# Linear-attention block with a gated MLP, on one core: operands' stages in the order of the products, wo's splits ahead of their matmuls, loads moved in the queue

## The chip, the core and the metric

One of the eight cores of a Trainium2 chip runs the whole program. The time is that of one launch on the device, in microseconds (us): the median of 3 runs of the kernel before is 2439.75 us (2436.82 to 2441.01). Engines are named as in the profile: PE is TensorE (matmuls; PEld its weight loads), DVE is VectorE, ACT is ScalarE, POOL is GpSimd, SP is SyncE, whose queue here issues nearly all loads.

## The reference

All tensors are float32; S = 2048 tokens, D = 1024, F = 3584, 32 heads of 32.

```python
xn   = layernorm(x)
q, k, v = heads(xn @ wqkv)                       # D x 3D
pq, pk  = phi(q), phi(k)                         # phi(t) = (t > 0 ? t + 1 : exp(t)) + 1e-6
kv   = einsum("bhsd,bhse->bhde", pk, v)
z    = pk.sum(over s)
o    = (pq @ kv) / (pq . z + 1e-6)
s    = rows(o) @ wo                              # D x D
h    = silu(xn @ w1) * (xn @ w3)                 # D x F each
out  = x + s * silu(h @ w2)                      # F x D
```

## The kernel before, in words

**Products.** A float32 operand is split by `split` (L79) into a high part, cast by ACT (L83), and the rest, subtracted by DVE (L84). `mm3` (L88) makes a product of three matmuls (L91 high × high, L92 high × low, L93 low × high). Each 2 × 2 block of a matrix product takes seven products in place of eight: the weights' operands are B11, T2, T3, T1, B21, T4, B22 in this order (`PRODUCTS`), with T1 = B12 − B11, T2 = B22 − T1, T3 = B22 − B12, T4 = B21 − T2, the activations' partners A11, S2, S3, S1, A12, A22, S4. One product of a projection is 12 matmuls of 128 × 512.

**The first era.** The tokens go in two halves of 1024. For each half `half` (L517) runs the groups k and v, then q, then gate and up (`g`, `u`; 14 pairs); `gemm` (L393) runs the seven products of one group and the sums on the results, such as c22 (L430, L436). Two groups can be run side by side, product by product (`paired`): the last gate/up pair of half 0 and the first k/v pair of half 1.

**What sets the order.** The code is traced in an order, and a scheduler then places the instructions by that order as a priority and by its own model of times; buffers come from pools with a fixed number of slots. Three streams are traced between the products of `gemm`:

- `next(stages)`, one stage a product: the stages of `Operands` (L281), which load a group's weights (raw tile, tag "raw") and make its seven split operands in the pool tag "b", of 8 slots. `ready` (L313) splits, `combine` (L319) subtracts in place over a raw quarter. `ask` (L292) loads; a group asks for the next group's weights as its own stages begin.
- `catch_up` (L381), one step of a job a product. In half 1 the jobs are `attention_work`: the denominators, `merge_wo` (for each of 8 row tiles of wo: multiply by the masked kv sums `kvm`, then the sums and the seven operands stored to `wp_d`), and `divide` (queries divided by the denominators, stored to `qs_d`). A job flagged `in_order` is issued no earlier than the loads in `fetched`.
- use of the results (`hidden`, `keys_values`): silu, the gate, stores to `h_d`, and sums stored to `hs_d`.

**Attention and layers.** A `Segment` holds seven operands of weights for each k (`right`) and runs over 8 groups m of 256 tokens. Attention multiplies the divided queries by `wp` (o @ wo merged), whose raw tiles `wpr` go through 2 buffers (loaded in `attention_right`, L1020). `operands(m + 1)` loads the queries (`left`, L953, 4 slots of tag "sg") while m runs. m = 0 takes each k's products as they land (`outer`). `late_work` (divide for m = 6 and 7) is the job of this phase. Then era 1's pools are closed and the layers B0 to B4 multiply h by w2 in the same way; their first raw tiles (`rB11B`, `rT2B`, ..., loaded at L970) use `small` (tag "c", 6 slots).

Names in the profile: `wos` is a split half of a wo tile, `wp` both the result of the merge (in the matmuls of L776) and attention's split operand; `XA11s` and so on are split queries; a trailing `s` or `B` stands for attention and a layer.

Of the kernel before, what the change touches and what calls it, by code (L numbers as in the profile page):

```python
# [16 lines left out]
P = 128  # L17
C = 512
# [4 lines left out]
def tile_linear_attention_times_swiglu(  # L23
# [27 lines left out]
    def bank(name):  # L51
        return ps.tile([P, C], F32, tag="bank", name=name)
# [228 lines left out]
    class Operands:  # L281
# [2 lines left out]

        def __init__(self, w, c0, name, early=False):
            self.w, self.c0, self.name, self.raw, self.next = w, c0, name, None, None
            self.B, self.places = {}, {}
            self.stages = self.made(early)  # L290

        def ask(self):  # L292
# [9 lines left out]
        def made(self, early):  # L302
            K = ND // 2
            b = {}

            def halves(t):
                b.update(B11=t[:, :K, :P], B21=t[:, K:, :P])

            def place(n):
                self.places[n] = pb.tile([P, 2, K, P], FR, tag="b", name=f"{n}{self.name}")  # L310

            def ready(n):
                if n not in self.places:  # L313
                    place(n)
                split(self.places[n], b[n])
                self.B[n] = self.places[n]
# [12 lines left out]
            self.ask()  # L329
            if self.next and not early:  # L330
                self.next.ask()
            halves(self.raw)
            b.update(B12=self.raw[:, :K, P:], B22=self.raw[:, K:, P:])
            if not early:
                ready("B11")
                yield
            combine("T1", "B12", "B11", "B11")
            ready("T1")
            if early:
                combine("T2", "B22", "T1", "T1")  # L340
                ready("T2")
            yield
            if not early:
                place("T2")
            combine("T3", "B22", "B12", "B12")
            ready("T3")
            yield
            if not early:
                ready("B21")
                yield  # L350
                combine("T2", "B22", "T1", "T1")
                ready("T2")
                yield
            combine("T4", "B21", "T2", "T2")
            ready("T4")
            yield
            ready("B22")
            yield

    def in_turn(groups):  # L360
# [393 lines left out]
    def merge_wo(k):  # L754

        both = []

        def load(e):
            j = k + e * (ND // 2)
            t = job_tile([P, 2, C], f"wo{j}")  # L760
            nc.sync.dma_start(out=t, in_=wo[j * P:(j + 1) * P, :].rearrange("p (n c) -> p n c", c=C))
            return t

        def steps(e, t):
            both.append(t)
            j = k + e * (ND // 2)
            f = small(f"kvf{j}")[:, :P]
            nc.vector.tensor_mul(f, hmask, kvacc[:, j])
            kvm = st.tile([P, 2, P], FR, tag="kvm", bufs=1, name=f"kvm{j}")
            split(kvm, f)  # L770
            for n in range(2):
                o = pb.tile([P, 2, C], FR, tag="b", name=f"wos{j}_{n}")
                split(o, t[:, n])
                yield True
                acc = bank(f"wp{j}_{n}")
                mm3(acc, (kvm[:, 0], kvm[:, 1]), (o[:, 0], o[:, 1]), True, True)  # L776
                nc.scalar.copy(out=t[:, n], in_=acc)
            yield True
            if e:
                b = [t[:, n] for t in both for n in range(2)]  # L780
                for n, i in (("B11", 0), ("B21", 2), ("B22", 3)):
                    store(n, b[i])
                yield from sums_of(*b)
                for n, i in (("T1", 0), ("T3", 1), ("T4", 2), ("T2", 3)):
                    store(n, b[i])
                for _ in range(3):
                    yield True

        def store(n, t):
            g, e = divmod(7 * k + PRODUCTS.index(n), 4)  # L790
            nc.sync.dma_start(out=wp_d[g][:, e], in_=t)

# [18 lines left out]

    groups = []
    for h in range(NH):
        some = [Operands(wqkv, part * D + pair * 2 * P, f"{'qkv'[part]}{h}_{pair}_", h == 0 and part and pair < 2)
                for parts in ((1, 2), (0,)) for pair in range(ND // 2) for part in parts]
        some += [Operands((w1, w3)[e], pair * 2 * P, f"{'gu'[e]}{h}_{pair}_") for pair in range(NF // 2) for e in range(2)]
# [7 lines left out]
    stages = in_turn(groups)  # L824
    for h in range(NH):
        half(h)
    jobs.append((late_work(), False))


    GT = 2 * P  # L830
# [106 lines left out]
    def left(m, g, halves, sums, nk, name, first=False):  # L937
# [7 lines left out]
        for e, n in enumerate(PRODUCTS):  # L945
            n = PARTNER[n]
            if first:
                if e % 2 == 0:
                    big = job_tile([P, 2, nk, P], f"r{e}{name}_{m}")
                t = big[:, e % 2]  # L950
            else:
                t = signed(f"r{n}{name}_{m}")[:, :nk * P].rearrange("p (k s) -> p k s", s=P)
            nc.sync.dma_start(out=t, in_=where[n])  # L953
            yield n, t

    def queries(m):
# [5 lines left out]
    def hiddens(i, m):  # L962
# [2 lines left out]
        return left(m, m % NT, [h_[:, :, e] for e in range(2)], [hs[:, :, e] for e in range(2)],  # L965
                    (FB[i][1] - FB[i][0]) // 2, f"B{i}")

    def second_weights(i, n, k):
        t = small(f"r{n}B{i}_{k}")
        nc.sync.dma_start(out=t, in_=second_weight(i, n, k))  # L970
        return t

    def second_weight(i, n, k):
        f0, f1 = FB[i]
# [16 lines left out]
        nc.vector.tensor_add(a, a, xs)  # L991
        nc.gpsimd.dma_start(out=out[r0:r0 + P, cols], in_=a)

    def run(seg, nxt=None, around=None):

        def between(k):
            if m == NG - 1 and nxt:
# [9 lines left out]
        for m in range(NG):  # L1007
            if m + 1 < NG:
                seg.operands(m + 1)
            seg.tokens(m, m == 0 or m == NG - 1 and nxt is not None, between)  # L1010


# [17 lines left out]
    attention.operands(0)  # L1030
    for k in range(attention.nk):
        attention.right(k)
    run(attention)
    assert all(next(j, None) is None for j, _ in jobs)
    jobs.clear()
    era1.close()
# [2 lines left out]
    def layer_place(n, i, k):  # L1039
# [36 lines left out]
```

## Time and profile before

| | |
|---|---|
| median of 3 runs | 2439.75 us |
| the profiled execution | 2441.47 us |
| its span, mean granted clock of PE | 2439.7 us, 0.988 |
| projections, gate and up | to about 1690 us; border of the halves near 840 |
| merging wo | within 1135 to 1300 us |
| attention | about 1690 to 1862 us |
| layers | from about 1862 us |
| DMA over the span | 408.63 MB, mean 167 GB/s |

A timeline row gives start, duration, engine, line, operation, out<-in, shapes, and in brackets the idle time before it with what ended it. `SPq` is SP's queue: the row is the issue of a load, which lands later. Two matmuls overlap, so a row of 0.39 us is followed by the next after 0.23.

### The profile page before, as it was taken

The numbers are of one execution on the slowest core, as the hardware profiler recorded it, in microseconds if no ns is written. First come the engines' busy times: TensorE is split into PE (matmuls) and PEld (weight loads), VectorE is DVE, ScalarE is ACT, GpSimd is POOL, SyncE is SP. The second block draws the span as 40 slices with busy tenths as digits, with TensorE's granted clock in tenths as the row PEclk, the third lists the DMA queues.
The fourth block names the chain that finished last, engine by engine and source line by source line (L and its number), as shares of the span: only waits on it lengthen the run. The fifth ranks groups of instructions, "written<-read, shape, count | busy, mean of one in ns | idle before, by whom it ended". The sixth has DMA issues, their size and how long they took to land.

```text
span 2439.7 us, 30863 instructions
## 1 busy us (share of the span) xinstructions
PE 2349.5 (96%) x10544; PEld 1934.8 (79%) x10544; DVE 1823.4 (75%) x2688; ACT 937.1 (38%) x1667; POOL 726.4 (30%) x909
## 2 busy tenths in 40 slices
PE   6999999999999999999989999999898999999997
PEld 5788888788888788887767888888686888777875
DVE  8655888888887755567778877888555776776797
ACT  4434644433233243354333323333323434343433
POOL 3000012256765200011324443234330032323253
PEclk9999999999999999999999999999999999999999
DMA  3211455576667731133455555457776445454597
GB/s 122 86 52 61 149 172 171 173 226 222 224 202 238 256 141 53 52 117 127 134 186 168 198 191 203 137 193 241 242 234 195 140 139 157 122 160 119 169 292 235
DMA packets 375134, 408.63 MB, mean 167 GB/s; under 512 B 19840, under 2 KB 308608, under 8 KB 374976
## 3 DMA queue, kind: packets, MB, share of 16 engines
q1 hardware_dynamic: 348800, 319.35, 42.2%
q0 software_dynamic: 26176, 87.31, 9.6%
q8 instruction: 82, 1.34, 0.2%
q14 instruction: 76, 0.62, 0.1%
HBM read 268.96 MB, written 137.63 MB: 167 GB/s over the span
## 4 chain that ended last, share of the span: by engine, by line
PE 50%; DVE 5%; DMA 4%; issue 3%; ACT 2%; POOL 0%; DVEq 0%; POOLq 0%; ACTq 0%; SPq 0%
PE dB L91 1%; PE dB L93 1%; PE dB L92 1%; DMA wpr<-wp_d 1%; PE cB L91 1%; PE cB L93 1%; PE cB L92 1%; PE aB L93 1%; PE aB L91 1%; PE aB L92 1%; PE den L713 1%; PE kv L506 1%; DMA rB11B<-in_B_w 1%; PE cs L92 1%; PE as L92 1%
## 5 line engine op out<-in xcount | busy, mean ns | idle before, releaser
L614 POOL DMA_DIRECT2D h_d<-sg x112 | 61.6, 550 | 364.3 <-DVE sg L613 359.9
L575 POOL DMA_DIRECT2D pq_d<-pq x32 | 17.4, 545 | 484.1 <-DVE pq L467 484.0
L912 POOL TENSOR_TENSOR acc<-acc,uB 128x512 f32<-128x512 f32 x25 | 41.6, 1665 | 157.7 <-DVE uB L909 157.7
L596 POOL TENSOR_TENSOR qd<-qd 128x128 f32<-128x128 f32 x32 | 25.2, 788 | 144.7 <-DVE qd L745 139.5
L889 POOL TENSOR_TENSOR acc<-acc,uB 128x512 f32<-128x512 f32 x7 | 11.7, 1676 | 147.0 <-ACT uB L881 147.0
L600 POOL TENSOR_TENSOR hs<-sg,hs 128x256 f32<-128x256 f32 x56 | 52.9, 945 | 1.6
L597 POOL TENSOR_TENSOR hs<-hs,sg 128x256 f32<-128x256 f32 x56 | 47.2, 842 | 0.0
L628 POOL TENSOR_TENSOR w<-w 128x256 f32<-128x256 f32 x28 | 26.0, 929 | 68.7 <-DMA w<-in_B_w 63.4
L982 POOL DMA_DIRECT2D s_d<-s x32 | 17.4, 544 | 94.1 <-DVE s L919 41.6
L599 POOL TENSOR_TENSOR hs<-sg 128x256 f32<-128x256 f32 x56 | 42.8, 765 | 0.0
L596 POOL TENSOR_TENSOR hs<-sg,sg 128x256 f32<-128x256 f32 x56 | 42.5, 759 | 1.0
L91 PE MATMUL cB<-T,XA22B 128*128 128x512 f32 x87 | 34.9, 401 | 7.5 <-DVE acc L916 7.2
L914 POOL TENSOR_TENSOR acc<-acc,uB 128x512 f32<-128x512 f32 x25 | 40.2, 1610 | 0.0
L83 ACT CAST XS4B<-rS4B 128x384 fp32r<-128x384 f32 (+1 forms) x40 | 19.6, 490 | 53.3 <-PE cB L93 45.0
L930 DVE TENSOR_TENSOR acc<-cB,acc 128x512 f32<-128x512 f32 x25 | 17.2, 687 | 29.4 <-PE cB L93 29.4
L989 ACT ACTIVATE acc<-acc 128x512 f32<-128x512 f32 x32 | 20.2, 632 | 48.1 <-DVE acc L919 15.2
L84 DVE TENSOR_TENSOR XS1B<-rS1B,XS1B 128x384 fp32r<-128x384 f32 (+1 forms) x40 | 36.5, 914 | 2.4 <-ACT XS1B L83 2.4
L83 ACT CAST XA11B<-rA11B 128x384 fp32r<-128x384 f32 (+1 forms) x40 | 19.7, 492 | 46.3 <-PE dB L93 28.4
L83 ACT CAST XS3B<-rS3B 128x384 fp32r<-128x384 f32 (+1 forms) x40 | 19.7, 492 | 45.6 <-DMA rS3B<-hs_d 17.3
L83 ACT CAST XS1B<-rS1B 128x384 fp32r<-128x384 f32 (+1 forms) x40 | 19.7, 493 | 45.4 <-PE cB L93 25.9
L91 PE MATMUL aB<-B,XA12B 128*128 128x512 f32 x87 | 34.2, 393 | 2.6 <-ACT uB L906 1.6
L506 PEld LDWEIGHTS kv<-kvr 128*128 128x128 f32 x256 | 33.5, 191 | 2.5
(5853 smaller groups left out, 8914.3 us busy)
## 6 DMA issues: line engine op xcount, KB each, us to landing
h_d<-sg POOLq DMA_DIRECT2D x112, 256.0 KB, 3.6
qs_d<-qd POOLq DMA_DIRECT2D x32, 512.0 KB, 3.8
hs_d<-hs POOLq DMA_DIRECT2D x60, 256.0 KB, 4.0
w<-in_B_w SPq DMA_DIRECT2D x56, 256.0 KB
wt_d<-w SPq DMA_DIRECT2D x28, 512.0 KB
hs_d<-hs SPq DMA_DIRECT2D x52, 256.0 KB
pq_d<-pq POOLq DMA_DIRECT2D x32, 256.0 KB, 3.2
a_dS<-xo SPq DMA_DIRECT2D x16, 512.0 KB
```

The costliest lines, as they stand in the source:

```text
L83: nc.scalar.copy(out=hi, in_=src)
L91: nc.tensor.matmul(acc, lhsT=wh, rhs=ah, start=start, stop=False, skip_group_check=True)
L92: nc.tensor.matmul(acc, lhsT=wh, rhs=al, start=False, stop=False, skip_group_check=True)
L93: nc.tensor.matmul(acc, lhsT=wl, rhs=ah, start=False, stop=stop, skip_group_check=True)
L506: nc.tensor.matmul(acc, lhsT=r[:, 1, t], rhs=r[:, 0, t], start=t == 0, stop=t == C // P - 1)
L596: nc.gpsimd.tensor_add(out=s1, in0=a21, in1=a22)
L597: nc.gpsimd.tensor_sub(out=s2, in0=s1, in1=a11)
L599: nc.gpsimd.tensor_sub(out=s3, in0=a11, in1=a21)
L600: nc.gpsimd.tensor_sub(out=s4, in0=a12, in1=s2)
L614: nc.gpsimd.dma_start(out=h_d[i][2 * h + c][:, 2 * k + n], in_=sg[n, c])
L912: G.tensor_add(out=c22, in0=c22, in1=u)
L914: G.tensor_add(out=c12, in0=c12, in1=u)
```

## The change

Five edits that leave the work as it is and move it.

1. `Operands`, groups after the first four: the stages were B11 | T1 | T3 | B21 | T2 | T4 | B22; they are B11 | T1 combined, T3 | T2 | T1 split | B21 | T4 | B22. T2 is now made over T3's raw quarter.
2. A flag `second` for the second group of each side-by-side pair: it asks for the next weights at the end of its stages instead of the start.
3. `merge_wo`: both halves of a wo tile are split first, a step each, then multiplied and copied, a step each. The trailing empty steps are cut from three to one.
4. `late_work` is flagged in order, and the queries' loads of m = 0 and 1 are put in `fetched`: its steps come after them.
5. `ask_first`, called when attention's last group begins: the first four raw tiles of layer B0 are loaded then, two of them into slots of tag "u"; B0's first weights are traced ahead of its first activations.

```diff
     class Operands:
-        def __init__(self, w, c0, name, early=False):
+        def __init__(self, w, c0, name, early=False, second=False):
...
-            if self.next and not early:
+            ahead = self.next is not None and not early
+            if ahead and not self.second:
                 self.next.ask()
...
+            if early:
...
+            else:
                 ready("B11")
                 yield
-            combine("T1", "B12", "B11", "B11")
-            ready("T1")
-            if early:
-                combine("T2", "B22", "T1", "T1")
+                combine("T1", "B12", "B11", "B11")
+                combine("T3", "B22", "B12", "B12")
+                ready("T3")
+                yield
+                combine("T2", "B22", "T1", "T3")
                 ready("T2")
-            yield
-            if not early:
-                place("T2")
-            combine("T3", "B22", "B12", "B12")
-            ready("T3")
-            yield
-            if not early:
+                yield
+                ready("T1")
+                yield
                 ready("B21")
-                yield
-                combine("T2", "B22", "T1", "T1")
-                ready("T2")
                 yield
             combine("T4", "B21", "T2", "T2")
             ready("T4")
             yield
             ready("B22")
+            if ahead and self.second:
+                self.next.ask()
             yield
@@ merge_wo
+            o = []
             for n in range(2):
-                o = pb.tile([P, 2, C], FR, tag="b", name=f"wos{j}_{n}")
-                split(o, t[:, n])
+                o.append(pb.tile([P, 2, C], FR, tag="b", name=f"wos{j}_{n}"))
+                split(o[n], t[:, n])
                 yield True
+            for n in range(2):
                 acc = bank(f"wp{j}_{n}")
-                mm3(acc, (kvm[:, 0], kvm[:, 1]), (o[:, 0], o[:, 1]), True, True)
+                mm3(acc, (kvm[:, 0], kvm[:, 1]), (o[n][:, 0], o[n][:, 1]), True, True)
                 nc.scalar.copy(out=t[:, n], in_=acc)
-            yield True
+                yield True
...
-                for _ in range(3):
-                    yield True
+                yield True
@@ after the two halves
-    jobs.append((late_work(), False))
+    jobs.append((late_work(), True))
@@ left
-            nc.sync.dma_start(out=t, in_=where[n])
+            load = nc.sync.dma_start(out=t, in_=where[n])
+            if name == "q" and m < 2:
+                fetched[:] = [load]
@@ layers' weights
+    asked = {}
+    def ask(i, n, k, place):
+        asked[i, n, k] = t = place(f"r{n}B{i}_{k}")
+        nc.sync.dma_start(out=t, in_=second_weight(i, n, k))
     def second_weights(i, n, k):
-        t = small(f"r{n}B{i}_{k}")
-        nc.sync.dma_start(out=t, in_=second_weight(i, n, k))
-        return t
+        if (i, n, k) not in asked:
+            ask(i, n, k, small)
+        return asked[i, n, k]
+    def ask_first():
+        for n, place in zip(PRODUCTS, (spare, spare, small, small)):
+            ask(0, n, 0, place)
+    def spare(name):
+        return pe.tile([P, C], F32, tag="u", name=name)
@@ run
             if m + 1 < NG:
                 seg.operands(m + 1)
+            elif ahead:
+                ahead()
...
-    run(attention)
+    run(attention, ahead=ask_first)
...
+    layers[0].right(0)
     layers[0].operands(0)
-    for k in range(layers[0].nk):
+    for k in range(1, layers[0].nk):
         layers[0].right(k)
```

ACT's order at the first tile of wo (`wos0_0` and `wos0_1` its two split halves, `wp0_0` and `wp0_1` the results that L777 copies back; `g1_1` is a gate group of half 1). Before:

```order
L83 CAST T1g1_1__9321<-wg1_1__9143 128x512
L719 COPY r1_9324<-den1_9043 32x512
L83 CAST wos0_0_9336<-wo0_9235 128x512
L83 CAST kvm0_9333<-kvf0_9331 128x128
L83 CAST T3g1_1__9357<-wg1_1__9143 128x512
L777 COPY wo0_9235<-wp0_0_9360 128x512
L83 CAST wos0_1_9365<-wo0_9235 128x512
L83 CAST B21g1_1__9382<-wg1_1__9143 128x512
L83 CAST T2g1_1__9355<-wg1_1__9143 128x512
L777 COPY wo0_9235<-wp0_1_9385 128x512
```

and with the change:

```order
L721 COPY r1_9325<-den1_9043 32x512
L83 CAST T3g1_1__9322<-wg1_1__9143 128x512
L83 CAST wos0_0_9337<-wo0_9235 128x512
L83 CAST kvm0_9334<-kvf0_9332 128x128
L83 CAST T2g1_1__9357<-wg1_1__9143 128x512
L83 CAST wos0_1_9360<-wo0_9235 128x512
L83 CAST T1g1_1__9377<-wg1_1__9143 128x512
L781 COPY wo0_9235<-wp0_0_9380 128x512
L83 CAST B21g1_1__9400<-wg1_1__9143 128x512
L83 CAST T4g1_1__9423<-wg1_1__9143 128x512
L409 COPY ug1_1__9495<-ag1_1__9496 128x512
L781 COPY wo0_9235<-wp0_1_9403 128x512
```

The second half's cast stood behind the copy of the first result; now two casts of the gate group's operands stand between the first half's cast and that copy, and both halves are ahead of it. T1's cast is behind T3's and T2's.

SP's queue at the last weights of attention (`wpr` raw weights, `qd6` a division's inputs for m = 6, `rA11q_1` and on the queries of m = 1). Before:

```order
L1020 DMA wpr4_13769<-wp_d4_128 128x1024 x2
L737 DMA qd6_0_14005<-r_d3_156 128x1x256
L739 DMA qd6_0_14005<-pq_d0_3_79 128x256
L737 DMA qd6_0_14005<-r_d3_156 128x1x256
L739 DMA qd6_0_14005<-pq_d1_3_83 128x256
L737 DMA qd6_1_14010<-r_d3_156 128x1x256
L1020 DMA wpr5_13781<-wp_d5_129 128x1024 x2
...
L1020 DMA wpr6_13793<-wp_d6_130 128x1024 x2
L739 DMA qd6_2_14075<-pq_d1_3_83 128x256
L953 DMA rA11q_1_13805<-qs_d1_146 128x4x128
```

and with the change:

```order
L1044 DMA wpr4_13769<-wp_d4_128 128x1024 x2
L1044 DMA wpr5_13781<-wp_d5_129 128x1024 x2
L1044 DMA wpr6_13793<-wp_d6_130 128x1024 x2
L958 DMA rA11q_1_13805<-qs_d1_146 128x4x128
L958 DMA rS2q_1_13810<-qs_d1_146 128x4x128
L958 DMA rS3q_1_13815<-qs_d1_146 128x4x128
L958 DMA rS1q_1_13820<-qs_d1_146 128x4x128
L958 DMA rA12q_1_13825<-qs_d1_146 128x4x128
L958 DMA rA22q_1_13830<-qs_d1_146 128x4x128
L958 DMA rS4q_1_13835<-qs_d1_146 128x4x128
L739 DMA qd6_0_14005<-r_d3_156 128x1x256
```

The division's loads moved from between the three weight groups to behind the queries of m = 1.

SP's queue where attention ends (`rS1q_7` queries of m = 7, `rS1B0_0` activations and `rB11B0_0` and so on weights of layer B0). Before:

```order
L953 DMA rS1q_7_14746<-qs_d7_152 128x4x128
L953 DMA rA12q_7_14751<-qs_d7_152 128x4x128
...
L953 DMA rS1B0_1_15108<-hs_d0_0_104 128x2x128
L970 DMA rB11B0_0_15015<-in_B_w2 128x512
L970 DMA rT2B0_0_15020<-wt_d0_131 128x512
L970 DMA rT3B0_0_15025<-wt_d0_131 128x512
L970 DMA rT1B0_0_15030<-wt_d0_131 128x512
L970 DMA rB21B0_0_15035<-in_B_w2 128x512
```

and with the change:

```order
L958 DMA rS1q_7_14746<-qs_d7_152 128x4x128
L980 DMA rB11B0_0_14870<-in_B_w2 128x512
L980 DMA rT2B0_0_14872<-wt_d0_131 128x512
L958 DMA rA12q_7_14751<-qs_d7_152 128x4x128
...
L958 DMA rS1B0_0_15030<-hs_d0_0_104 128x2x128
L980 DMA rT3B0_0_14874<-wt_d0_131 128x512
L980 DMA rT1B0_0_14876<-wt_d0_131 128x512
```

Two of the four first weights moved ahead of attention's last three query loads, the other two ahead of the layer's later activations.

More of the change, by code (lines that the diff above doesn't have):

```diff
@@ L281, in tile_linear_attention_times_swiglu @@
     class Operands:
-        def __init__(self, w, c0, name, early=False):
+        def __init__(self, w, c0, name, early=False, second=False):
             self.w, self.c0, self.name, self.raw, self.next = w, c0, name, None, None
-            self.B, self.places = {}, {}
+            self.B, self.second = {}, second
             self.stages = self.made(early)
@@ L307, in halves @@
                 b.update(B11=t[:, :K, :P], B21=t[:, K:, :P])
-            def place(n):
-                self.places[n] = pb.tile([P, 2, K, P], FR, tag="b", name=f"{n}{self.name}")
             def ready(n):
[L313 to L316, printed above, removed]
+                self.B[n] = pb.tile([P, 2, K, P], FR, tag="b", name=f"{n}{self.name}")
+                split(self.B[n], b[n])
             def combine(n, i0, i1, there):
@@ L333, in made @@
             b.update(B12=self.raw[:, :K, P:], B22=self.raw[:, K:, P:])
-            if not early:
+            if early:
+                combine("T1", "B12", "B11", "B11")
+                ready("T1")
+                combine("T2", "B22", "T1", "T1")
+                ready("T2")
+                yield
[3 more added lines that the diff above has]
+            else:
                 ready("B11")
                 yield
-            combine("T1", "B12", "B11", "B11")
-            ready("T1")
-            if early:
-                combine("T2", "B22", "T1", "T1")
-                ready("T2")
-            yield
-            if not early:
-                place("T2")
-            combine("T3", "B22", "B12", "B12")
-            ready("T3")
-            yield
-            if not early:
+                combine("T1", "B12", "B11", "B11")
+                combine("T3", "B22", "B12", "B12")
+                ready("T3")
+                yield
+                combine("T2", "B22", "T1", "T3")
+                ready("T2")
+                yield
+                ready("T1")
+                yield
                 ready("B21")
-                yield
-                combine("T2", "B22", "T1", "T1")
-                ready("T2")
                 yield
@@ L813, in tile_linear_attention_times_swiglu @@
     for h in range(NH):
-        some = [Operands(wqkv, part * D + pair * 2 * P, f"{'qkv'[part]}{h}_{pair}_", h == 0 and part and pair < 2)
+        some = [Operands(wqkv, part * D + pair * 2 * P, f"{'qkv'[part]}{h}_{pair}_", h == 0 and part and pair < 2,
+                         h and part == 2 and pair == 0)
                 for parts in ((1, 2), (0,)) for pair in range(ND // 2) for part in parts]
-        some += [Operands((w1, w3)[e], pair * 2 * P, f"{'gu'[e]}{h}_{pair}_") for pair in range(NF // 2) for e in range(2)]
+        some += [Operands((w1, w3)[e], pair * 2 * P, f"{'gu'[e]}{h}_{pair}_", second=h == 0 and e and pair == NF // 2 - 1)
+                 for pair in range(NF // 2) for e in range(2)]
         ends = some[:2 * h], some[2 * h:len(some) - 2 * (1 - h)], some[len(some) - 2 * (1 - h):]
@@ L992, in finish, with run @@
         nc.gpsimd.dma_start(out=out[r0:r0 + P, cols], in_=a)
-    def run(seg, nxt=None, around=None):
+    def run(seg, nxt=None, ahead=None):
         def between(k):
```

## The prediction

> **What bounds the kernel now.** I read the page's busy row first, then a table by stages, then TensorE's waits, then the timelines around the longest of them.
>
> ```profile
> PE 2349.5 (96%) x10544; PEld 1934.8 (79%) x10544; DVE 1823.4 (75%) x2688; ACT 937.1 (38%) x1667; POOL 726.4 (30%) x909
> ```
>
> TensorE is the bound: 96% busy. No part of the change removes a matmul, so a gain can only come out of time in which TensorE waits or runs at the lower clock. Where that time lies is shown by the view of windows (length, busy time and count of PE, PEld, DVE, ACT, POOL, then the granted clock, DMA share and GB/s):
>
> ```profile
> 1135.00:1300.00 165.00, 145.74 (x603) 114.62 (x602) 122.77 (x153) 58.63 (x109) 46.93 (x53) 0.96 0.45 149
> 1690.00:1730.00 40.00, 30.54 (x115) 22.94 (x114) 26.25 (x36) 14.91 (x27) 11.51 (x19) 0.87 0.84 259
> 1850.00:1905.00 55.00, 47.12 (x192) 36.38 (x191) 38.61 (x72) 25.00 (x52) 2.16 (x4) 0.94 0.68 210
> 840.00:870.00 30.00, 27.46 (x107) 21.51 (x106) 21.63 (x29) 8.45 (x15) 10.04 (x14) 0.89 0.98 368
> 1300.00:1690.00 390.00, 390.00 (x1722) 322.92 (x1722) 323.56 (x412) 133.03 (x226) 157.26 (x242) 1.00 0.57 188
> ```
>
> The last row is the undisturbed stage: 390.00/1722 = 0.2265 us a matmul, so a product of 12 matmuls, one place of the order, takes 2.72 us. At this pace the other windows should take 603 × 0.2265 = 136.6, 26.0, 43.5 and 24.2 us; they take 28.4, 14.0, 11.5 and 5.8 us more, 59.7 together. They are the stages that the change touches: merging wo, the start of attention, the first layer's start and the border between the halves. What PE waits for there (us in total, times, longest):
>
> ```profile
> PE wp L91 <- ACT wos L83: 11.4, 8, 4.5
> ...
> PE T1s L91 <- ACT wp L83: 5.6, 1, 5.6
> ...
> PE wp L92 <- DVE wos L84: 3.2, 1, 3.2
> PE B11B L91 <- ACT B L83: 2.9, 1, 2.9
> PE B22s L91 <- ACT wp L83: 2.8, 1, 2.8
> ...
> PE cg__3944 L91 <- DVE c22g__3987 L430: 2.0, 1, 2.0
> ...
> PE wp L91 <- ACT kvm L83: 1.8, 1, 1.8
> ...
> PE bk__7103 L91 <- ACT T2k__6952 L83: 0.9, 1, 0.9
> ```
>
> The waits are less than the loss, since a long one is followed by a slow stretch. From the timeline of TensorE (start, duration):
>
> ```profile
> 1723.06 0.80 PE L91 MATMUL T1s<-wp,XS1s 128*128 128x512 f32 x1 [5.64 <-ACT wp L83]
> ...
> 1725.88 0.63 PE L91 MATMUL T4s<-wp,XA22s 128*128 128x512 f32 x1
> ...
> 1726.67 0.40 PE L92 MATMUL T4s<-wp,XA22s 128*128 128x512 f32 x1
> ```
> ```profile
> 474.26 0.50 PE L91 MATMUL cg__3944<-A,T4g__3859 128*128 128x512 f32 x1 [1.96 <-DVE c22g__3987 L430]
> ...
> 475.71 0.39 PE L91 MATMUL cg__3944<-A,T4g__3859 128*128 128x512 f32 x1
> 475.94 0.40 PE L92 MATMUL cg__3944<-A,T4g__3859 128*128 128x512 f32 x1
> ```
>
> After a wait of 5.64 us nine matmuls start between 1723.06 and 1726.67, 8 steps in 3.61 us where the full pace takes 1.81: 1.8 us lost besides the wait. After one of 1.96 us the steps are 0.23 us again. So a long wait shortened below 2 us saves more than its length.
>
> **The change part by part.** Counts of matmuls, splits, copies and loads stay; only places move. So each term is a wait taken away or made.
>
> *Merging wo.* Before, a half of wo is split one place (2.72 us) ahead of its matmuls; the second half's split is put behind the copy of the first result.
>
> ```profile
> 1147.83 0.62 ACT L83 CAST wos<-wo 128x512 fp32r<-128x512 f32 x1
> ```
> ```profile
> 1148.51 0.50 PE L91 MATMUL wp<-wos,kvm 128*128 128x512 f32 x1 [1.37 <-ACT wos L83]
> ```
> ```profile
> 1262.58 3.27 DVE L768 TENSOR_TENSOR kvf<-hmask,kvacc 128x128 f32<-128x128 f32 x1
> ```
> ```profile
> 1262.93 0.73 POOL L596 TENSOR_TENSOR hs<-sg,sg 128x256 f32<-128x256 f32 x1
> ...
> 1264.97 0.71 POOL L597 TENSOR_TENSOR hs<-hs,sg 128x256 f32<-128x256 f32 x1
> ```
> ```profile
> 1267.08 0.61 ACT L83 CAST wos<-wo 128x512 fp32r<-128x512 f32 x1
> ```
> ```profile
> 1267.75 0.80 PE L91 MATMUL wp<-wos,kvm 128*128 128x512 f32 x1 [4.55 <-ACT wos L83]
> ```
>
> The first pair is the second half's: cast ends, matmul starts. The other rows are the worst case: VectorE's small mask product takes 3.27 us beside GpSimd's sums of 1262.93 to 1265.68, the cast comes after it, TensorE stands 4.55 us. The waits on wos and kvm sum to 11.4 + 3.2 + 1.8 = 16.4 us. With both halves split two places ahead, each gets one more product, 2.72 us: of 4.5 there stays 1.8, of 3.2 0.5, of the others (all below 2.72) nothing: 14.1 saved. What the window lost beyond those waits is 28.4 − 16.4 = 12.0; the long waits' slow stretches and the restarts are in it, and about half, 6, should go with them. I take 20. Bounds: 10, if half of the lead is eaten by work put ahead of the split, and 28, all of the window's loss. The two tiles now stay a place longer in the eight shared slots; that is the third rival.
>
> *Late divisions behind the query loads.* SP's queue, ScalarE's and VectorE's timelines:
>
> ```profile
> 1695.71 0.81 SPq L1020 DMA_DIRECT2D wpr<-wp_d  x2
> ...
> 1700.52 1.34 SPq L1020 DMA_DIRECT2D wpr<-wp_d  x2
> ...
> 1711.12 1.71 SPq L1020 DMA_DIRECT2D wpr<-wp_d  x2
> ```
> ```profile
> 1701.20 1.14 ACT L83 CAST wp<-wpr 128x512 fp32r<-128x512 f32 x2 [3.32 <-DMA wpr<-wp_d]
> ...
> 1722.39 1.14 ACT L83 CAST wp<-wpr 128x512 fp32r<-128x512 f32 x2 [8.91 <-DMA wpr<-wp_d]
> ```
> ```profile
> 1706.79 1.28 DVE L84 TENSOR_TENSOR wp<-wpr,wp 128x512 fp32r<-128x512 f32 x2
> ```
>
> Three weight groups go through two raw buffers. The last (1711.12) needs the buffer that VectorE gives back at 1706.79 + 1.28 = 1708.07; it is issued 3.05 us later because loads for divide 6 stand before it, and lands 11.3 us after issue, where the first landed in 5.5 (1695.71 to 1701.20). Now these three stand together and the division's loads behind seven loads of queries. Issue at 1708.1 and landing in 5.5 give 1713.6 instead of 1722.4. TensorE got to T1s at 1723.06 − 5.64 = 1717.4, so the 5.6 us wait goes; with 1.8 of slow stretch 7.4. I take 7. Lower bound 3: only the issue's 3 us is won and the landing stays at 11 us since the queries' loads take the division's place on the DMA. Upper 11: the 2.8 us wait on B22s and a further restart go too. The division of tokens 6 and 7 is late next; a token group is seven products, 7 × 2.72 = 19 us, and the query loads of group 6 are called for during group 5, five groups or 95 us on, which covers it. If that cover failed, m = 6 would wait for one landing, 5.5 us.
>
> *First weights of the layer asked in attention.*
>
> ```profile
> 1860.04 0.55 SPq L970 DMA_DIRECT2D rB11B<-in_B_w  x1
> ```
> ```profile
> 1863.26 0.62 ACT L83 CAST B<-rB11B 128x512 fp32r<-128x512 f32 x1 [1.76 <-DMA rB11B<-in_B_w]
> ...
> 1868.65 0.62 ACT L83 CAST B<-rB21B 128x512 fp32r<-128x512 f32 x1
> ```
>
> The first tile is issued at 1860.04 and cast at 1863.26; five tiles are cast in 5.4 us, about 1.1 us apiece, as they land. Four of the first seven now land before the attention's end, so the fifth can be about 4 us earlier, and the 2.9 us before the first product is gone. The rest of the seven still lands at that pace beside a product phase that takes 0.68 us for each tile (3 matmuls), so part of the wait comes back there: I take 4, with 1 (the wait moves to the fifth tile) and 8 (most of the 11.5) as bounds. SP carries two of the loads ahead of the last three query loads; at 0.55 us each this costs their issue 1.1 us, beside products of 2.72 us.
>
> *Order of the stages, and the flag second.* The splits now stand in the order in which the products use them. At the halves' border T2 was late (its 0.9 us row), and the second load now goes behind the activations that both pairs need. I take 4.5 of the 5.8 us, with 0 and 5.8 as bounds. In the steady stage there is nothing to win: PE is full. There T1 gives up lead:
>
> ```profile
> 1369.63 0.69 DVE L84 TENSOR_TENSOR T1g__11022<-wg__10851,T1g__11022 128x512 fp32r<-128x512 f32 x1
> ```
> ```profile
> 1390.49 0.39 PE L91 MATMUL dg__11192<-S,T1g__11022 128*128 128x512 f32 x1
> ```
>
> From 1370.3 to 1390.5 are 20.2 us; two places later leave 20.2 − 5.4 = 14.8. That is cover enough, and costs nothing.
>
> *A cost.* Moved splits can put VectorE's epilogue sums (c22) behind them where two products on one accumulator follow closely. Before, such a wait cost 2.0 us at its worst (the c22 row). I allow for three, −6.
>
> Sum: 20 + 7 + 4 + 4.5 − 6 = 29.5 us off the profiled execution's 2441.5 (span 2439.7): 2412.0. The profiled one stands 1.7 above the median of 2439.75, so on the median's basis 2410.3, say 2410. All upper bounds without the cost: 28 + 11 + 8 + 5.8 = 52.8, 2387; all lower: 10 + 3 + 1 + 0 − 6 = 8, 2432.
>
> **The rivals.** *Waits stay because VectorE is held up (GpSimd).* The row of 3.27 us at 1262.58 ends with GpSimd's run of sums (1265.85 against 1265.68), and the lead is time on VectorE too: with two halves' splits close together, more of VectorE falls under such a run. Against it: VectorE is busy 122.77 of 165, and one more product is nearly as long as the stretch. It leaves half of the merge (10), of attention (3.5) and of the start (2), and 3 at the border: 18.5 − 6 = 12.5 off, 2427. The Trainium skill, "SBUF — State Buffer", section "SBUF: two separate sides", says that VectorE and GpSimd share a port pair as an exclusive lock, and that a VectorE instruction with two SBUF inputs is blocked for the whole of a GpSimd one that reads SBUF. By that rule, every split from a raw tile is exposed whatever its place; the trace agrees with it in the 3.27 us row.
>
> *Slower: operands starve.* From split to use a half of wo holds one of the eight slots a place longer, and the second half is split while the first still holds its own. If the shared ring of slots is full, the operands behind come one place late for each of the two, 5.4 us a job. Over 8 jobs 43.5 us stand against 29.5 gained: 14 slower, 2454. It decides from 29.5/8 = 3.7 us a job. Against it: lead of the operands is 14.8 us for T1 after the change, more than the 5.4 taken.
>
> *No change to speak of.* The time won is given to the next wait: attention's second token group waits for query loads, and merged halves for GpSimd's stores, so that TensorE arrives early and stands. Only the border's 4.5 us less a 2 us wait remain, 2437.5; what a measurement of this kernel can tell from no change is about 0.2%, 4.9 us. Against it: from 1300 to 1690 TensorE has no idle time to be late into.
>
> **How the numbers follow.** Forecast 0.65 (2410; its own range 2396 to 2421), held-up VectorE 0.20 (2427), no change 0.08 (2437), starved operands 0.07 (2454). Faster 0.65 + 0.20 = 0.85, same 0.08, slower 0.07. The range of 8 in 10 takes the forecast's own and the second case, and leaves the all-gains end and the last two out: 2394 to 2430.
>
> **What would show it.** Right: wos and kvm waits of TensorE below 4 us in sum; wpr6 issued within 1 us of its buffer's release, and no wait on T1s over 1 us; no wait of B11B; the window of the merge at 0.99 of the clock. Wrong: waits on g or u operands (T1 above all) in the merge; rows of VectorE's casts over 2.5 us ahead of a wp wait; the first wait in attention gone to XA11s of the second token group; new waits on c22 above 6 us in sum.

## The result, and the profile after

The changed kernel takes 2419.32 us (median of 4 runs, 2415.15 to 2424.34) against 2439.93 before (4 runs): ratio 0.9921, 95% interval 0.9906 to 0.9935, so 20.6 us or 0.8% faster. The forecast was 2410 within 2394 to 2430. The profiled execution is the slowest of the four, 2424.34 us (span 2422.6, clock 0.991), 17.1 below the profiled one before.

The same windows as before (fixed times, so each holds a slightly later piece of the program):

```profile
488.00:793.00 305.00, 297.83 (x1304) 245.35 (x1303) 247.83 (x291) 95.48 (x162) 186.74 (x240) 0.99 0.66 219
840.00:870.00 30.00, 27.91 (x117) 22.59 (x116) 21.89 (x28) 9.13 (x17) 9.56 (x15) 0.94 1.05 392
1135.00:1300.00 165.00, 160.43 (x694) 130.74 (x693) 130.94 (x174) 64.66 (x119) 52.67 (x60) 0.99 0.49 164
1690.00:1730.00 40.00, 32.02 (x122) 23.94 (x121) 28.47 (x37) 15.06 (x26) 12.49 (x21) 0.91 0.78 250
1850.00:1905.00 55.00, 51.20 (x212) 39.89 (x211) 42.18 (x83) 25.50 (x57) 0.00 (x0) 0.97 0.62 189
```

The merge (third row) now holds 694 matmuls where it held 603. The start of attention is hardly better (122 after 115). And a row that the prediction did not watch is worse: 488 to 793, gate and up of half 0, held 1347 matmuls in 305.00 us of busy TensorE before, and holds 1304 now.

```profile
488.00:793.00 305.00, 305.00 (x1347) 252.52 (x1347) 261.41 (x297) 99.83 (x166) 190.31 (x240) 1.00 0.67 222
```

(That row is of the kernel before.) TensorE's waits after the change:

```profile
PE cs L91 <- DVE s L921: 5.1, 1, 5.1
PE cg__10225 L91 <- DVE c22g__10259 L432: 3.5, 1, 3.5
...
PE cg__5225 L91 <- DVE c22g__5257 L432: 3.3, 1, 3.3
PE cg__3945 L91 <- DVE c22g__3987 L432: 2.8, 1, 2.8
...
PE bk__7101 L93 <- DVE T2k__6953 L84: 2.1, 1, 2.1
PE cg__4281 L91 <- DVE c22g__4313 L432: 2.0, 1, 2.0
PE cg__4597 L91 <- DVE c22g__4629 L432: 1.9, 1, 1.9
...
PE wp L91 <- ACT wos L83: 1.0, 3, 0.5
```

The waits on wos and kvm are 1.0 us (16.4 before), and T1s and B11B are gone from the head of the list. At the border the wait on T2 is not gone: it was 0.9 us for ScalarE's cast and 1.0 for VectorE's half of the split, and is 2.1 for VectorE's half alone. New are waits on VectorE's sums: c22 of gate groups (one of 2.0 us, at the place of cg__3945, stood there before), and `s` in attention. All of these hold the next product on the same accumulator bank: in the program it may write there only once VectorE has read the bank.

To place gains and losses I took from each trace the start of TensorE's n-th matmul record (10544 in every kernel) and subtracted that of the kernel before. The table gives what each stage adds, in us; minus is time won. It sets one execution beside one other, so a few us of a row can be chance. Names of the runs are those of the experiments below.

| stage (time before) | after | hybrid | late3 | nosum | nosum1 | spread | orderonly | plainorder | mergeonly | mergeask | poolq | noload |
|---|---|---|---|---|---|---|---|---|---|---|---|---|
| half 0, gate and up (488–793) | +9.7 | 0.0 | +4.6 | 0.0 | +6.4 | +7.8 | +5.6 | 0.0 | 0.0 | +0.1 | 0.0 | 0.0 |
| border (840–870) | −2.2 | −2.2 | −3.7 | −6.2 | −2.2 | −3.8 | −1.2 | −0.2 | −1.1 | −1.2 | −4.6 | −1.4 |
| merge (1135–1310) | −20.6 | −20.7 | −20.6 | −20.6 | −26.0 | −20.6 | +0.7 | −24.9 | −24.9 | −24.9 | −24.8 | −24.9 |
| attention's group 0 (1310–1732) | −7.2 | −7.4 | −7.2 | −9.1 | −13.5 | −7.1 | +3.1 | −10.8 | −1.1 | −1.6 | −4.6 | −8.4 |
| attention's groups 1 to 7 (1732–1860) | +6.7 | +6.4 | +6.6 | +7.8 | +4.2 | +5.8 | 0.0 | +7.6 | 0.0 | 0.0 | 0.0 | 0.0 |
| layer's start (1860–1905) | −3.1 | −5.4 | −2.7 | −4.9 | −5.5 | −1.7 | −1.2 | −4.9 | 0.0 | −3.9 | −5.0 | −5.0 |

### The profile page after: what moved, and what is told of

It reads as the page before. It is cut to its first block, busy times and chain, and to the rows that moved or that the text cites. A ratio compares the mean times of both kernels' runs of the same rounds, so it can differ in the third digit from the quotient of the medians.

```text
span 2422.6 us, 30793 instructions
## 1 busy us (share of the span) xinstructions
PE 2343.7 (97%) x10544; PEld 1932.8 (80%) x10544; DVE 1804.7 (74%) x2688; ACT 934.6 (39%) x1667; POOL 723.7 (30%) x909
## 4 chain that ended last, share of the span: by engine, by line
PE 49%; DVE 6%; DMA 5%; issue 3%; ACT 1%; POOL 1%; DVEq 0%; SPq 0%; POOLq 0%; ACTq 0%
PE dB L91 1%; PE dB L93 1%; PE dB L92 1%; PE cB L91 1%; PE cB L93 1%; PE cB L92 1%; PE aB L93 1%; PE aB L91 1%; PE aB L92 1%; DMA rA11B<-h_d 1%; PE den L715 1%; PE kv L508 1%; DMA wpr<-wp_d 1%; PE bB L93 1%; PE bB L92 1%
## 5 line engine op out<-in xcount | busy, mean ns | idle before, releaser
L1011 ACT ACTIVATE acc<-acc 128x512 f32<-128x512 f32 x32 | 20.2, 633 | 43.7 <-DVE acc L924 14.8
L91 PE MATMUL dB<-B,XS4B 128*128 128x512 f32 x87 | 34.4, 395 | 1.2 <-DVE acc L924 1.2
```

The lines of the kernel that those rows point to most:

```text
L91: nc.tensor.matmul(acc, lhsT=wh, rhs=ah, start=start, stop=False, skip_group_check=True)
```

## The experiments

Two theories were set against each other for each of the two new waits. For c22: the new order of the stages puts more of VectorE's work ahead of the sum, or GpSimd stretches VectorE wherever the stages stand. For attention: the division's loads stand between the query loads in SP's queue, or the transfers or slots are the limit.

**hybrid: the old order in half 0.** The edit: single groups of half 0 keep the old stages; all else as changed.

```diff
+            elif self.plain:                      # h == 0, but not its last pair
+                ready("B11"); yield
+                combine("T1", ...); ready("T1"); yield
+                place("T2"); combine("T3", ...); ready("T3"); yield
+                ready("B21"); yield
+                combine("T2", ...); ready("T2"); yield
             else:
                 ready("B11")
```

> The changed kernel, but the single groups of half 0 (queries, gate and up except the last pair) make their stages in the old order (T1, T3, B21, T2); half 1, the border's pairs and the other edits stay. Theory (the new order is late on VectorE in half 0, because two subtractions now stand ahead of the first split, so the c22 sum of T3 comes after TensorE wants its bank): the c22 waits on gate groups of half 0 fall from 10 us (3.3, 2.8, 2.0, 1.9) to 2 us as before the change, and the time falls by 8 to 10 us to about 2410. Rival (VectorE is stretched by GpSimd wherever the stages stand): waits of 6 us or more stay there, and the time stays at 2417 to 2421.

Measured 2411.82 us (ratio 0.9884, 0.9869 to 0.9899). The wait list of 488 to 793 is empty, and the stage's loss is 0.0 in place of +9.7. So the order is needed for the loss. What it changed is seen on VectorE around one group, first in the kernel before, then after:

```profile
624.91 1.11 DVE L84 TENSOR_TENSOR T3u__5241<-wu__5032,T3u__5241 128x512 fp32r<-128x512 f32 x1
625.94 0.68 DVE L430 TENSOR_TENSOR c22g__5257<-cg__5224,ug__5202 128x512 f32<-128x512 f32 x1
```
```profile
628.58 2.29 DVE L84 TENSOR_TENSOR T3u__5219<-wu__5032,T3u__5219 128x512 fp32r<-128x512 f32 x1 [0.74 <-ACT T3u__5219 L83]
630.91 1.29 DVE L315 TENSOR_TENSOR wu__5032<-wu__5032 128x512 f32<-128x512 f32 x1
632.13 0.68 DVE L425 TENSOR_TENSOR ug__5202<-bg__5224,ug__5202 128x512 f32<-128x512 f32 x1
632.97 1.10 DVE L84 TENSOR_TENSOR T2u__5241<-wu__5032,T2u__5241 128x512 fp32r<-128x512 f32 x1 [0.17 <-ACT T2u__5241 L83]
634.10 3.27 DVE L315 TENSOR_TENSOR wu__5032<-wu__5032 128x512 f32<-128x512 f32 x1
637.30 0.68 DVE L432 TENSOR_TENSOR c22g__5257<-cg__5225,ug__5202 128x512 f32<-128x512 f32 x1
```

Before, the c22 sum follows T3's split at once. After, T2's split and the next subtraction, 3.27 us long, stand between (and an earlier sum, `ug`): c22 starts at 637.30, and TensorE has waited 3.28 us for it.

**nosum: without GpSimd's sums in half 0.** The four sums on each pair of h tiles are left out in half 0 and the tiles stored in their place.

```diff
         def sums(c):
+            if h == 0:
+                for e in range(2):
+                    nc.gpsimd.dma_start(out=hs_d[i][2 * h + c][:, k, e], in_=sg[e, c])
+                return
```

> The changed kernel without GpSimd's four sums on each pair of h tiles in half 0: the h tiles themselves are stored in their place, so the layers' sums operands of half 0 hold other data. If GpSimd beside VectorE is needed for the c22 waits of half 0, they fall below 2 us in sum, VectorE's rows of 3 us in 488 to 793 are gone, and that window holds some 40 matmuls more than the 1302 of the changed kernel. If the amount of VectorE's work and its order alone do it, 6 us or more of these waits stay.

Measured 2405.05 us (one run). No wait is left in the window, and it holds 1347 matmuls, as many as before the change, in spite of the new order. VectorE's busy time there falls from 247.83 to 212.53 us for 291 and 299 instructions:

```profile
488.00:793.00 305.00, 305.00 (x1347) 252.53 (x1347) 212.53 (x299) 100.13 (x166) 132.34 (x176) 1.00 0.68 221
```

So GpSimd is needed as well: each theory named one of two conditions, and both must hold. The costliest subtractions on raw weights, in the changed kernel and in this one, show the stretch:

```profile
L315 DVE TENSOR_TENSOR wu__5032<-wu__5032 128x512 f32<-128x512 f32 x4 | 7.8, 1958 | 0.1
```
```profile
L315 DVE TENSOR_TENSOR wg__4192<-wg__4192 128x512 f32<-128x512 f32 x4 | 3.2, 798 | 0.1
```

A mean of 1958 ns with the sums beside it, 798 ns at most without.

**nosum1: the same in half 1.** The edit above with `h == 1`, on the queue that half 1 uses.

> The changed kernel without GpSimd's four sums on each pair of h tiles in half 1 (the h tiles are stored in their place, so half 1 of the layers' sums holds other data). If VectorE's split of T4 (5.8 us) and its subtraction (3.0 us) ahead of the 3.5 us wait on c22 in the merge are stretched by GpSimd's sums, both are below 1.5 us, that wait is below 0.5 us, and the merge wins 24 us in place of 20. Half 0 keeps its loss of 5 to 10 us. If not, the 3.5 us stay.

Measured 2404.63 us (one run). The 3.5 us wait in the merge is gone and the merge wins 26.0 us in place of 20.6; half 0 still loses 6.4. What held the merge in the changed kernel is seen on VectorE and GpSimd:

```profile
1247.10 5.80 DVE L84 TENSOR_TENSOR T4g__10124<-wg__9839,T4g__10124 128x512 fp32r<-128x512 f32 x1 [2.17 <-ACT T4g__10124 L83]
```
```profile
1247.18 1.29 POOL L631 TENSOR_TENSOR wo<-wo,wo 128x512 f32<-128x512 f32 x1
1248.42 0.73 POOL L599 TENSOR_TENSOR hs<-hs,sg 128x256 f32<-128x256 f32 x1
1249.12 1.28 POOL L633 TENSOR_TENSOR wo<-wo,wo 128x512 f32<-128x512 f32 x1
1250.37 0.72 POOL L602 TENSOR_TENSOR hs<-sg,hs 128x256 f32<-128x256 f32 x1
1251.06 1.28 POOL L634 TENSOR_TENSOR wo<-wo 128x512 f32<-128x512 f32 x1
```

A split that takes 0.68 us alone takes 5.80, to 1252.90. GpSimd's run of sums began at 1245.78; its last five, shown, lie beside the split and end at 1252.34. In nosum1, with the hs sums left out and the sums of wo still there, the same split takes 1.43 us:

```profile
1243.91 1.43 DVE L84 TENSOR_TENSOR T4g__10100<-wg__9815,T4g__10100 128x512 fp32r<-128x512 f32 x1 [2.17 <-ACT T4g__10100 L83]
```

The Trainium skill, "SBUF — State Buffer", section "SBUF: two separate sides", calls the port pair that the two engines share an exclusive lock, held for a whole instruction. The trace agrees in kind; it shows more than one instruction's length, since the split did not end before the fifth was over.

**spread: the two subtractions in two stages.** T1's subtraction moves behind B11's split.

```diff
             else:
                 ready("B11")
+                combine("T1", "B12", "B11", "B11")
                 yield
-                combine("T1", "B12", "B11", "B11")
                 combine("T3", "B22", "B12", "B12")
```

> The changed kernel with T1's subtraction moved one stage ahead, behind B11's split, so that no stage has two subtractions; the order of the splits stays the new one. If the pair of subtractions in one stage is what makes c22 late, the c22 waits of half 0 fall from 10 to below 3 us and the time to about 2410. If it is the amount of work that stands ahead of the c22 sum (three subtractions and two splits in any case), 6 us or more of waits stay: 2415 to 2424.

Measured 2421.41 us (ratio 0.9931, 0.9916 to 0.9946): no better than the changed kernel. Waits of 8.4 us in half 0 stay (3.3, 2.8, 2.3). It is not the pair of subtractions in one stage; it is what stands ahead of c22 altogether.

**orderonly: the order alone on the kernel before.** The edits 1 and 2 and nothing else.

> The kernel before with the new order of Operands' stages and the flag second alone. By the difference of the changed kernel and the run named plainorder, the order is a loss: about 10 us in half 0 (c22 waits on gate groups), 2 us won at the border, up to 4 us lost by c22 in the merge: slower than before by 6 to 12 us, 2446 to 2452. Rival (its cost exists only together with the other edits, or lies within the spread of the runs): 2436 to 2443, with waits on c22 in half 0 of 3 us at most.

Measured 2447.61 us (ratio 1.0044, 1.0030 to 1.0059): the order by itself makes the kernel slower by 10.4 us. The ledger gives +5.6 for half 0, less than the 9.7 of the changed kernel; the runs with the new order and all sums in half 0 range from 4.6 to 9.7 there. Attention's start loses another 3.1. The loss expected in the merge does not show without the merge's edit (+0.7). The rows of the ledger add up to 7.0, the medians differ by 10.4.

**plainorder: the order undone.** The changed kernel with the old `Operands`.

> The changed kernel with Operands as before the change in both halves (old stage order, no flag second); merging wo, late divisions and the layer's first loads as changed. If the merge's gain belongs to wo's earlier splits alone, TensorE's drift over 1135 to 1300 stays at about -20 us, half 0 wins 10 and the border loses 2: about 2411. If the merge needs the new order of stages as well (T2 and the slots are too tight in the old one), half or more of the 20 us is lost, and waits on g and u operands or on wos of 8 us or more show there: 2420 or more.

Measured 2406.12 us (ratio 0.9867, 0.9852 to 0.9881), 13 us below the changed kernel on medians, lower than either side expected. Half 0's loss is gone, and the merge wins 24.9 us, more than with the new order: it needs no help from it. The border is −0.2 here. But poolq and mergeask, with the same old order at the border, have −4.6 and −1.2: the border moves by several us from run to run, and the 2.2 us of the changed kernel cannot be told from that (the last section shows what moves it).

**mergeonly: the merge's edit alone.**

> The kernel before with the edit to the merge of wo alone. Theory (the merge's gain is that edit's own, and nothing downstream takes it back): TensorE's matmuls are 24 to 25 us earlier after the merge and stay so to the end, waits on wos and kvm fall from 16.4 to about 2 us, time 2414 to 2416. Rival (part of the gain belongs to the first loads and late divisions, because the attention's weights must land earlier too): the wait on T1s at the start of attention grows from 5.6 us by a good part of the 24, and the time is 2420 or more.

Measured 2415.72 us (ratio 0.9902, 0.9887 to 0.9916), as the theory had it. The waits on wos are 2.1 us and T1s still waits 5.2:

```profile
PE T1s L91 <- ACT wp L83: 5.2, 1, 5.2
```

One stage wins 24.9 us and the others of the table stay within 1.1. This edit alone is worth at least as much as the five together (24.6 us against 20.6; the two intervals overlap).

**late3: the division's loads behind the queries of group 2 as well.**

```diff
-            if name == "q" and m < 2:
+            if name == "q" and m < 3:
```

> The changed kernel, but the late divisions' steps wait for the query loads of groups 0, 1 and 2 instead of 0 and 1. Theory (the 5.1 us wait of cs for VectorE's sum in group 1 comes from the split of XS3s of group 2 ahead of it, whose load was issued among the division's loads at 1716.1 and landed at 1723.9): the wait on L921 is below 1 us, the six queries' issues of group 2 follow each other, and the time falls by 5 to 7 us to about 2413. Rival (the loads are bound by the transfers or by the four slots of the queries, not by their neighbours in the queue): a wait of 3 us or more stays in groups 1 or 2, the time stays at 2417 to 2421.

Measured 2422.76 us (ratio 0.9938, 0.9921 to 0.9955): no gain; the theory's number failed. In the changed kernel the chain had been this, on SP, ScalarE, VectorE and TensorE:

```profile
1710.81 0.55 SPq L958 DMA_DIRECT2D rA11q<-qs_d  x1
1711.40 0.66 SPq L739 DMA_DIRECT2D qd<-r_d  x1
...
1715.07 0.90 SPq L741 DMA_DIRECT2D qd<-pq_d  x1
1716.06 0.54 SPq L958 DMA_DIRECT2D rS3q<-qs_d  x1
```
```profile
1723.86 0.62 ACT L83 CAST XS3s<-rS3q 128x512 fp32r<-128x512 f32 x1 [3.78 <-DMA rS3q<-qs_d]
```
```profile
1724.51 0.69 DVE L84 TENSOR_TENSOR XS3s<-rS3q,XS3s 128x512 fp32r<-128x512 f32 x1 [3.71 <-ACT XS3s L83]
1725.12 0.68 DVE L921 TENSOR_TENSOR s<-cs,us 128x512 f32<-128x512 f32 x1
```
```profile
1725.86 0.80 PE L91 MATMUL cs<-wp,XA22s 128*128 128x512 f32 x1 [5.10 <-DVE s L921]
```

The sum needs no query of group 2; it stands behind its split on VectorE. With m < 3 the queries of group 2 go first and twelve division loads follow in one row, issued from 1714.17 to 1722.03. Group 3's first query is issued after them (1723.46), its queries land late, and a copy of the group before stands behind their casts on ScalarE:

```profile
1730.82 0.62 ACT L83 CAST XA11s<-rA11q 128x512 fp32r<-128x512 f32 x1 [12.08 <-DMA rA11q<-qs_d]
1734.04 0.62 ACT L83 CAST XS2s<-rS2q 128x512 fp32r<-128x512 f32 x1 [2.60 <-DMA rS2q<-qs_d]
1734.56 0.58 ACT L911 COPY us<-as 128x512 f32<-128x512 f32 x1
```

TensorE waits 4.1 us for that copy.

So postponing these loads in SP's queue hands the wait on. Whether the place in the queue or the transfers cause it was left to the next two.

**poolq: the division's loads through GpSimd's queue**, on plainorder.

```diff
+            queue = nc.gpsimd if m >= LATE else nc.sync
...
-                nc.sync.dma_start(out=t[:, 2 + e], ...)
-                nc.sync.dma_start(out=t[:, e], ...)
+                queue.dma_start(out=t[:, 2 + e], ...)
+                queue.dma_start(out=t[:, e], ...)
```

> The run named plainorder with the late divisions' loads issued on GpSimd's queue instead of SP's. Theory (the 5.1 us wait of cs in group 1 comes from the division's loads standing between the query loads in SP's queue): SP issues the queries of group 2 back to back, the wait is below 1 us, and with the slow stretch after it 6 to 7 us are won: 2399 to 2400. Rival (the transfers themselves are the limit: the DMA is busy 85 to 92% between 1700 and 1720): query tiles land as late as before and a wait of 3 us or more stays: 2404 to 2408.

Measured 2400.64 us (ratio 0.9842, 0.9823 to 0.9861), the fastest version, 39.6 us under the kernel before. The wait on `s` is gone; of groups 0 and 1 there stays

```profile
PE T2s L92 <- DVE wp L84: 2.0, 1, 2.0
PE as L91 <- ACT XA11s L83: 1.7, 1, 1.7
PE T2s L91 <- ACT wp L83: 0.8, 1, 0.8
```

But the edit moved more than the queue. The first twelve of these loads now start ahead of every query of m = 1 (from 1686.63), where plainorder has them among the queries, from 1695.37 to 1712.56:

```profile
1666.56 0.72 POOL L738 DMA_DIRECT2D qd<-r_d  x1
...
1678.34 0.57 POOL L740 DMA_DIRECT2D qd<-pq_d  x1 [0.48 <-DMA qd<-pq_d]
```

So this run does not tell the place in SP's queue from the transfers. Both may count: rS3q of the chain above was not only issued late, it was also cast 7.80 us after its issue, against 3.54 us here (1701.04 to 1704.58). By the ledger attention wins 1.4 us over plainorder (−4.6 against −3.2), and the border 4.4, which this edit does not touch. A cleaner pair for the queue is mergeask, below: there the same twelve loads stand in SP's queue at nearly the same time (1668.93 to 1684.63), the last weights are issued at 1683.00 in place of 1674.01, T1s waits 4.8 us, and attention stands at −1.6, 3.0 us behind poolq.

**noload: no loads for the late divisions**, on plainorder; their tiles are set to one.

```diff
+            if m >= LATE:
+                nc.gpsimd.memset(t, 1.0)
+                return t
```

> The run named plainorder without the loads of the late divisions: their tiles are filled with ones on GpSimd, so the queries of groups 6 and 7 are not those of the reference; the products and stores stay. Both the queue's places and the transfers are gone. If the loads are the cause of the wait of cs in group 1 by either way, it falls below 1 us and some 7 us are won (2399). If 4 us or more stay, the cause lies elsewhere: in the four slots for queries or in the stores.

Measured 2400.51 us (one run), as poolq. By the ledger attention stands at −8.4 here and at −4.6 in poolq, so the loads on GpSimd's queue still cost some 4 us in group 0; poolq has 3.2 us more at the border, which varies. Place and transfers are both gone here, so the loads are shown to be the cause of group 1's wait; which of the two it was stays open.

**mergeask: plainorder without the late divisions' move.**

> The kernel before with the merge edit and the layer's first loads, without the late divisions' move and without the new stage order; it differs from the run named plainorder by the late divisions' move alone. If that move wins at T1s what it loses at the sum of group 1, as the ledger of plainorder says (11 us won to the end of group 0, 7.7 us lost in group 1), the time is 1 to 5 us above plainorder's 2406. If the move costs nothing else and its gain of 7 us is whole, 2413. If it is a loss, 2403 or less.

Measured 2409.32 us (ratio 0.9877, 0.9863 to 0.9892), 3.2 above plainorder, inside the 1 to 5 that the ledger's reading gave. Attention as a whole (groups 0 to 7) stands at −1.6 here and at −10.8 + 7.6 = −3.2 in plainorder: by these figures the move is worth 1.5 to 3 us, not 7, and the intervals of the two runs overlap.

## Why the prediction was right, and where not

Sign and range held. The median is 9 us above the forecast. Two terms were too favourable, late divisions and the allowance for c22; a third, the merge, was put too low and hides part of that.

- **Merging wo: the mechanism right, the size partly luck.** 20 forecast, 20.6 measured. The rest on wos and kvm was put at 2.3 us and is 1.0; mergeonly shows the edit earning it alone. But the 20.6 is net. With the old order the edit earns 24.9, within the bound of 28, and 4.3 of it went to the c22 cost below.
- **Late divisions: the step that failed.** The forecast's 7 us "so the 5.6 us wait goes" came true: the last weights are issued at 1696.09, when VectorE gives their buffer back (1694.79 + 1.28), and their first half is cast 4.8 us later; T1s waits 0.4 us at most, and group 0 takes 7.2 us less. (The 2.8 us on B22s went as well, and 1.6 us on VectorE's split for the first product came.) But 6.7 came back within group 1. The step asked what is late next and answered with the division's own use, 95 us off. It did not ask who stands behind the moved loads in SP's queue: the queries of group 2, and through their split the sum of group 1. The rival "no change to speak of" did name the query loads of the second token group as the next wait; the late load was that of the third. Net 0.5.
- **Layer's start: 4 forecast, 3.1 measured;** the wait before the first product fell from 2.9 to 0.9 us (B11B's second matmul, on VectorE). The runs with this edit and no stretch at the lower clock there win 3.9 to 5.5. The working had a slip: five casts in 5.4 us are four steps, 1.35 us apiece and not 1.1, so the fifth tile could be 5.4 us earlier.
- **Border: 4.5 forecast, 2.2 seen, not shown to be the change's.** Kernels with the old order there vary from −0.2 to −4.6. The reason given failed: T2 is still what TensorE waits for, 2.1 us in the changed kernel and 2.6 in orderonly, since VectorE's half of its split comes late (2.99 us long in the changed kernel). In nosum that half takes 0.68 us and no wait is left in the window (−6.2).
- **The allowance for c22: mis-sized.** It was 6 us; half 0 alone cost 9.7, and the merge another 4.3 (24.9 against 20.6), 14 in all. The allowance took three waits at the one 2.0 us row. Five came on gate groups, 13.5 us in sum where one of 2.0 had stood (the prediction's own sign of being wrong was 6 us of new ones); they go up to 3.5, and two were followed by a slow stretch.
- **"In the steady stage there is nothing to win" was true, and nothing to lose was not.** The argument weighed T1's lead (14.8 us left), and T1 was never late: the list shows no wait on g or u operands. What was late was a result's sum, queued behind the operands that now come sooner. A cover must be reckoned for each engine's queue, not for the moved operand alone.
- **The rivals.** VectorE held up by GpSimd (0.20) was the mechanism of the shortfall, but in another place than its sentence said: not on the splits of wo, whose waits fell to 1.0 us, but on c22 behind the weights' splits. Its 2427 is 8 above the result, the forecast 9 below. Starved operands did not show. The loss came from the order, as that rival's side had it, but by another chain.

The sum of the ledger, for the profiled executions: −20.6 − 0.5 − 3.1 − 2.2 + 9.7 = −16.7 of the profiled difference of −17.1; the rest lies at the start and in the layers.

## What to carry to other kernels

When operands are made earlier on an engine that also reads the results off, count what now stands ahead of each result's sum, and how long that work is beside the neighbour that stretches it; the lead of the moved operand says nothing of it. When loads are moved back in a queue, look at who is now behind them, then at whose instruction is queued behind that tile's split. Another queue was better here than a later place, but it also moved the loads in time. Of several edits made at once, undo each: here one was worth 25 us, one some 4, one 2 or 3, and one cost 10 to 13.

## What the runs showed that was not expected

How long TensorE waits does not alone decide whether it runs slowly afterwards. In the changed kernel a wait of 2.00 us is followed by steps of 0.43 us (the prediction had taken 1.96 us as harmless), and one of 3.28 us by steps of 0.23:

```profile
516.62 0.50 PE L91 MATMUL cg__4281<-A,T4g__4194 128*128 128x512 f32 x1 [2.00 <-DVE c22g__4313 L432]
...
517.74 0.63 PE L91 MATMUL cg__4281<-A,T4g__4194 128*128 128x512 f32 x1
518.17 0.63 PE L92 MATMUL cg__4281<-A,T4g__4194 128*128 128x512 f32 x1
```
```profile
638.03 0.50 PE L91 MATMUL cg__5225<-A,T4g__5137 128*128 128x512 f32 x1 [3.28 <-DVE c22g__5257 L432]
638.37 0.39 PE L92 MATMUL cg__5225<-A,T4g__5137 128*128 128x512 f32 x1
638.60 0.39 PE L93 MATMUL cg__5225<-A,T4g__5137 128*128 128x512 f32 x1
```

The traces record the granted clock, and that shows what decides. Between 100 us and the last 20 us of the 13 traces it falls to 0.50 in 55 stretches, of 3.41 or 6.83 us each, and within a trace all of them start on one grid of 3.413 us. Cut at the grid, the two waits look like this (window, length, PE busy and count, then the other engines as before, granted clock, DMA share and GB/s):

```profile
513.63:517.04 3.41, 1.41 (x7) 0.86 (x6) 3.37 (x6) 2.18 (x4) 0.40 (x1) 1.00 0.84 265
517.04:520.45 3.41, 3.41 (x10) 2.64 (x9) 3.37 (x5) 0.63 (x1) 2.50 (x4) 0.50 0.86 262
```
```profile
633.08:636.50 3.42, 1.67 (x8) 1.05 (x6) 3.39 (x2) 0.90 (x2) 3.40 (x6) 1.00 0.38 147
636.50:639.91 3.41, 1.88 (x8) 1.57 (x9) 3.28 (x5) 0.65 (x2) 1.38 (x2) 1.00 0.00 0
639.91:643.32 3.41, 3.41 (x17) 2.83 (x16) 1.89 (x3) 2.24 (x4) 0.00 (x0) 1.00 0.00 0
```

The 2.00 us fall into one window, and the next one runs at half the clock. The 3.28 us are parted between two, 1.75 and 1.53, and neither is followed by a slow one. Over the 13 traces each of the 41 windows at full clock with 1.96 us idle or more was followed by a slow one; of those with 1.51 to 1.90 us 14 of 40 were, and of those with less none. A slow window with TensorE busy costs half its length, 1.7 us. Where the grid lies differs from trace to trace (slow windows behind the wait on cg__4281 start at 517.04 in the changed kernel and at 516.5 in spread), so such a cost can come and go between runs of nearly the same kernel. At the border it does: the kernel before and plainorder have two slow windows there, late3, nosum, poolq and spread none, the other seven one, and the ledger's row follows (−0.2; −3.7 to −6.2; −1.1 to −2.2).

The Trainium skill, "TensorE: Matmul & The Clock Gate", section "What's actually happening", has the lower clock come after at least one idle window of about 3.4 us and lets the window run free of the kernel's start. The grid agrees with the second; the first is more than these traces need, where 1.96 us of idling in one window was always enough.
